# The output layer of four units by seven block products, with sums on VectorE and later operands

## Chip, core and metric

The kernel runs on one core of one Trainium2 chip. The metric is the device time of one execution in microseconds (us). TensorE (PE in the profile) multiplies, ScalarE (ACT) and VectorE (DVE) read its results from PSUM, GpSimd (POOL) works on SBUF alone, and SyncE (SP) issues nearly all DMAs.

## What is computed

Attention inside chunks of 64 rows, then a layer that takes the greatest of three products, then an output layer, all in float32:

```python
# q, k, v: (8, 8, 576, 64); chunks of 64 rows
scores = q_c @ k_c.T / 8;  attn = softmax(scores);  x = attn @ v_c   # x: 4608 x 512
h = np.maximum(np.maximum(x @ w1, x @ w2), x @ w3)                   # 4608 x 768
out = h @ w_out                                                       # 4608 x 512
```

A float32 product is made of three TensorE passes over operands that are split in a high and a low part (function `three`): low times high, high times low, high times high. So each operand costs a copy to the high part (ScalarE) and a subtraction for the low part (VectorE).

## The kernel before

The 4608 rows are 36 tiles of 128. Two groups of four tiles come first; a written order (`FIRST`) runs the first of them beside the weights' loading. The other 28 tiles form four units of 6, 8, 8 and 6 tiles (`UNITS`); I call them units 0 to 3. A unit has a hidden layer and an output layer.

The hidden layer of a unit is done by seven block products in place of eight, for nine sets (three pairs `jp` of hidden blocks, times w1, w2, w3): the tokens of the unit are two halves, the 512 inputs two halves, the pair of hidden blocks two halves. `product(n, i)` makes product `i` of set `n`; the order is 1, 7, (3 of the set before), 6, 2, 4, 5. The seven weight operands of each set are mixed once (`store`) and kept in DRAM, from where `load` brings them to a ring. The seven operands made of the unit's x are made once per unit (`operands`): four differences (`mix`, VectorE makes two and GpSimd two), seven high parts (ScalarE) and seven low parts (VectorE). They are made while TensorE still works on the output layer of the unit before, since the unit's products all need them. Product 6 adds onto the bank of product 1, after ScalarE has copied product 1 out (`kept`).

When w is 2, the greatest values are final: `operand` splits them in a high part (`H`, line 535) and a low part (line 539), 12 pairs per unit, spread over the hidden layer.

The output layer (`project`, line 596) runs plainly: for each tile of 128 tokens six blocks of 128 hidden units, three matmuls of 512 columns each; then ScalarE copies the bank (line 586) and SyncE stores it. Product 3 of the last set runs inside it.

All engines follow one order that the program writes out: `plan(at, pe, fn)` puts a piece of work into a heap with a due time, `passed(step)` advances a clock by the length of each group of matmuls and issues all that is due. So an engine's order is fixed when the program is built, and each engine takes its instructions strictly in that order. `insertion` puts the attention of two further tiles between the matmuls: scores, softmax (VectorE and ScalarE, the scaling by the sum on GpSimd for units 1 to 3), a transpose and the products with v.

Of the kernel before, what the change touches and what calls it, by code (L numbers as in the profile page):

```python
# [9 lines left out]
F32 = mybir.dt.float32  # L10
# [24 lines left out]
OPERANDS, SLOWER = (0.3, 2.0), (1.0, 1.8)  # L35
# [28 lines left out]
def chunk_attn_maxout_kernel(  # L64
# [119 lines left out]
    def three(o, ah, al, bh, bl, first, last, onto=False):  # L184
        nc.tensor.matmul(out=o, lhsT=al, rhs=bh, start=first and not onto, stop=False, skip_group_check=onto)  # L185
        nc.tensor.matmul(out=o, lhsT=ah, rhs=bl, start=False, stop=False, skip_group_check=onto)  # L186
        nc.tensor.matmul(out=o, lhsT=ah, rhs=bh, start=False, stop=last, skip_group_check=onto)  # L187
# [258 lines left out]

    def unit(t0, count, rooms, turn):
# [4 lines left out]
        hh, hl = [None] * JT, [None] * JT  # L452
        stage, m, s = rooms["stage"], rooms["m"], rooms["s"]
# [6 lines left out]
        def room(n):  # L460
            return lambda: s()[:, 2 * n:2 * n + 2, :half]

        b11, b21, b12, b22 = (block(k, c) for c in range(2) for k in range(2))
        source = {1: b11, 2: b21, 3: b22, 4: room(0), 5: room(0), 6: room(1), 7: b12}
# [4 lines left out]
        def high(i):  # L469
            def fn():  # L470
                X[i] = rooms["X"](i)[:, :, :, :half]
                nc.scalar.copy(out=X[i][:, 0], in_=source[i]())
            return fn
# [4 lines left out]
        def operands():  # L478
            return [(0.0, high(1)), (0.6, low(1)), (1.0, high(2)), (1.6, mix(5, b12, b11, nc.vector)), (2.6, low(2)),
                    (2.7, high(5)), (3.6, mix(6, b22, source[5], nc.vector)), (3.7, mix(7, b22, b12, nc.gpsimd)),  # L480
                    (4.6, low(5)), (4.7, high(6)), (5.6, low(6)), (5.8, high(3)), (5.9, mix(4, b21, source[6], nc.gpsimd)),
                    (6.6, low(3)), (6.8, high(7)), (7.6, low(7)), (8.4, high(4)), (9.4, low(4))]
# [20 lines left out]

        def product(n, i):

            jp, w = sets[n]
            a, b = 2 * jp, 2 * jp + 1
            p7 = 2 + 2 * (n % 2)

            def M(j, c):  # L510
                return m()[:, j - a, c, :half]

            def reads(fn):
                def last():
                    fn()
                    give(place)
                return last

            def copy(to):
                return lambda: nc.scalar.copy(out=to, in_=o)  # L520

            def value(k, j, c):
                return lambda: nc.vector.tensor_tensor(out=o if w else M(j, c), in0=o, in1=kept(k), op=plus)  # L523

            def fourth():
                nc.gpsimd.tensor_tensor(out=kept(3) if w else M(b, 1), in0=kept(3), in1=kept(p7), op=plus)  # L526

            def greater(j, c, of):
                return lambda: nc.vector.tensor_tensor(out=M(j, c), in0=of, in1=M(j, c), op=most)  # L529

            def high(j, c):
                def fn():
                    if hh[j] is None:
                        hh[j], hl[j] = (rooms["H"](2 * j + k) for k in range(2))
                    nc.scalar.copy(out=hh[j][:, c * half:(c + 1) * half], in_=M(j, c))  # L535
                return fn

            def low(j, c):
                return lambda: nc.vector.tensor_tensor(out=hl[j][:, c * half:(c + 1) * half], in0=M(j, c),  # L539
                                                       in1=hh[j][:, c * half:(c + 1) * half].bitcast(F32), op=minus)  # L540

            def operand(at, j, c):
                return [(at, high(j, c)), (at + 0.9, low(j, c))] if w == 2 else []

            def summed(k, j, c):
                if w == 0:
                    return [(0.25, reads(value(k, j, c)))]
                return [(0.25, value(k, j, c)), (0.9, reads(greater(j, c, o)))] + operand(2.3, j, c)

            key = n, chain[i]  # L550
            begins = i in (1, 7, 2)
            if begins:
                bank, place = take()
                chains[key] = bank[:, :half], place
            o, place = chains[key]
            if i in (1, 6, 7):
                after = [(0.25, copy(kept({1: 0, 6: 1, 7: p7}[i])))]
            elif i == 5:
                after = [(0.25, copy(kept(3))), (1.2, fourth)]
                after += [(2.5, greater(b, 1, kept(3)))] if w else []  # L560
                after += operand(4.0, b, 1)
            elif i == 2:
                after = summed(0, a, 0)
            elif i == 4:
                after = summed(1, b, 0)
            else:
                after = [(0.25, reads(greater(a, 1, o) if w else copy(M(a, 1))))] + operand(1.6, a, 1)
            for k in range(2):
                hi, lo = weights(n, i, k)
                three(o, hi, lo, X[i][:, 0, k, :half], X[i][:, 1, k, :half], k == 0, k == 1, not begins)  # L570
                yield step, after if k else []
# [9 lines left out]
        def output(tt, of, place):  # L581
            outputs.append(tt)
            o = ao_p.tile([P, DO], F32, name="ao", tag=f"ao{len(outputs) % 4}")
            rows = out[(t0 + tt) * P:(t0 + tt + 1) * P, :]
            if t0 + tt < NT - 1:
                nc.scalar.copy(out=o, in_=of)
                give(place)
                nc.sync.dma_start(out=rows, in_=o)
                return
            left, right = slice(0, 256), slice(256, 512)  # L590
            nc.scalar.copy(out=o[:, left], in_=of[:, left])
            nc.vector.tensor_copy(out=o[:, right], in_=of[:, right])
            nc.scalar.dma_start(out=rows[:, left], in_=o[:, left])
            nc.sync.dma_start(out=rows[:, right], in_=o[:, right])

        def project(*tts, before=JT):
            o, at = {}, {}
            for js in (range(before), range(before, JT)):
                for tt in tts:
                    for j in js:  # L600
                        if j == 0:
                            o[tt], at[tt] = take()
                        cols = slice(tt * P, (tt + 1) * P)
                        three(o[tt], hh[j][:, cols], hl[j][:, cols], woh[:, j, :], wol[:, j, :], j == 0, j == JT - 1)
                        yield STEP, [(0.3, lambda tt=tt: output(tt, o[tt], at[tt]))] if j == JT - 1 else []
                    if tt == 0 and 0 in js and before < JT:
                        yield from product(len(sets) - 1, 3)

        return dict(operands=operands, load=load, hidden=hidden, project=project)
# [94 lines left out]
    H_AT = [(hpool, f"h{k}") for k in range(6)] + [("late", f"k{k}") for k in range(3)]  # L704
    H_AT += [(att, "aa"), (att, "qs"), (att, "rv")]

    def H(k):
        pool, tag = H_AT[k]
        return (late["hold"] if pool == "late" else pool).tile([P, 2 * HALF], F32R, name="H", tag=tag, bufs=1)

    def X(i):
        return hold(("X", i), lambda: late["hold"].tile([P, 2, 2, 512], F32R, name=f"X{i}"))

    rooms = dict(
        stage=stage, X=X, H=H,
        m=lambda: hold("m", lambda: late["hold"].tile([P, 2, 2, HALF], F32, name="most")),
# [72 lines left out]
    def operands(u):  # L789
        if u < len(units):  # L790
            for at, fn in units[u][0]["operands"]():
                plan(now + OPERANDS[min(u, 1)] + SLOWER[min(u, 1)] * at, 0.0, fn)
# [13 lines left out]
    for u, (it, t0, count) in enumerate(units):  # L806
        time = (len(sets) * 14 - 2) * STEP_H[count] + (1.15 if u else 1.65) * sum(UNITS[u + 1:u + 2])
        parts.append(("do", lambda u=u, time=time: series(u + 1, time, 12.0 if u == 0 else 9.0)))
        for n in range(len(sets)):
# [61 lines left out]
```

## Time and profile before

| | |
|---|---|
| Median of 3 runs | 622.86 us (622.02 to 623.68) |
| Profiled execution | 623.29 us, its span 621.5 us |
| PE busy | 612.5 us, 99% of the span |
| DVE, ACT, POOL busy | 59%, 43%, 28% |
| Granted TensorE clock | 1.000 |
| Output layer of units 0, 1, 2, 3 begins at | 250.58, 369.5, 493.7, 592.2 us |

The profile's busy share of PE counts an issued matmul until its modelled end, so starts of consecutive rows give its pace. A group row gives a line, engine, operation, shapes, count, the summed and the mean time, and the idle time ahead of them.

### The profile page before, as it was taken

What the parts mean: (1) busy time and instruction counts of PE and PEld (TensorE: products, weight loads), DVE (VectorE), ACT (ScalarE), POOL (GpSimd) and SP (SyncE); (2) the same over time, 40 slices, a digit from 0 to 9 for tenths busy, and PEclk for the clock granted to TensorE, in tenths of its full rate; (3) what the DMA queues carried; (4) which work ended last, traced back from release to release, by engine and by line L of the source; (5) the groups of instructions that cost most, each with busy time, mean ns of one, the idle gap of its engine ahead of it and who ended that gap; (6) DMA issues with size and microseconds to landing.
All of it is one profiled execution on the core that took longest, in us unless ns stands there. A gap on an engine that the chain in (4) does not pass through costs nothing.

```text
span 621.5 us, 12425 instructions
## 1 busy us (share of the span) xinstructions
PE 612.5 (99%) x5046; PEld 524.5 (84%) x5046; DVE 369.5 (59%) x581; ACT 268.2 (43%) x470; POOL 175.0 (28%) x150
## 2 busy tenths in 40 slices
PE   7899999999999999999999999999999999999997
PEld 3888878887899999888888888888888888999986
DVE  4898965777937665955675669336374480245330
ACT  4887644434444444453344344243343441333321
POOL 2522576786412202422121215002020130111100
PEclk9999999999999999999999999999999999999999
DMA  8987668764958868546788783557758621577402
GB/s 335 359 307 275 234 187 308 257 240 163 373 203 292 322 249 294 201 161 229 253 300 278 255 272 135 170 179 230 253 178 281 215 74 68 185 260 265 138 20 82
DMA packets 56264, 141.06 MB, mean 227 GB/s; under 512 B 5392, under 2 KB 21008, under 8 KB 56208
## 3 DMA queue, kind: packets, MB, share of 16 engines
q1 hardware_dynamic: 56064, 140.14, 63.8%
q8 instruction: 40, 0.66, 0.4%
q14 instruction: 16, 0.13, 0.1%
q10 hardware_dynamic: 144, 0.13, 0.1%
HBM read 110.62 MB, written 29.62 MB: 226 GB/s over the span
## 4 chain that ended last, share of the span: by engine, by line
PE 92%; DVE 6%; ACT 1%; issue 1%; POOL 0%; DVEq 0%; ACTq 0%; POOLq 0%
PE pm L185 28%; PE pm L186 28%; PE pm L187 28%; PE s L235 2%; PE pm L294 2%; PE tp L258 1%; PE pm L660 1%; DVE e L245 1%; DVE s L426 1%; DVE sm L193 1%; DVE mx L240 1%; DVE sm L196 0%; POOL c L418 0%; DVE m L349 0%; DVE xl L305 0%
## 5 line engine op out<-in xcount | busy, mean ns | idle before, releaser
L185 PE MATMUL pm<-X,ring 128*128 128x512 f32 (+1 forms) x504 | 184.2, 365 | 0.0
L187 PE MATMUL pm<-X,ring 128*128 128x512 f32 (+1 forms) x504 | 182.4, 362 | 0.0
L186 PE MATMUL pm<-X,ring 128*128 128x512 f32 (+1 forms) x504 | 182.3, 362 | 0.0
L520 ACT COPY kept<-pm 128x384 f32<-128x384 f32 (+1 forms) x144 | 76.7, 534 | 137.0 <-PE pm L187 134.0
L185 PEld LDWEIGHTS pm<-X,ring 128*128 128x128 f32 x504 | 94.6, 188 | 10.5
L186 PEld LDWEIGHTS pm<-X,ring 128*128 128x128 f32 x504 | 94.7, 188 | 9.8
L187 PEld LDWEIGHTS pm<-X,ring 128*128 128x128 f32 x504 | 94.6, 188 | 9.8
L526 POOL TENSOR_TENSOR kept<-kept 128x384 f32<-128x384 f32 (+1 forms) x24 | 27.7, 1155 | 151.0 <-ACT kept L520 151.0
L523 DVE TENSOR_TENSOR pm<-pm,kept 128x384 f32<-128x384 f32 (+1 forms) x48 | 30.2, 629 | 67.2 <-PE pm L187 67.1
L187 PE MATMUL pm<-woh,H 128*128 128x512 f32 x168 | 65.4, 390 | 0.0
L186 PE MATMUL pm<-wol,H 128*128 128x512 f32 x168 | 65.4, 390 | 0.0
L185 PE MATMUL pm<-woh,H 128*128 128x512 f32 x168 | 65.3, 389 | 0.0
L185 PE MATMUL pm<-xh,wl 128*128 128x512 f32 (+1 forms) x156 | 60.1, 385 | 0.0
L186 PE MATMUL pm<-xl,wh 128*128 128x512 f32 (+1 forms) x156 | 58.4, 374 | 0.3 <-DVE xl L305 0.3
L187 PE MATMUL pm<-xh,wh 128*128 128x512 f32 (+1 forms) x156 | 58.3, 374 | 0.0
L529 DVE TENSOR_TENSOR most<-pm,most 128x384 f32<-128x384 f32 (+1 forms) x72 | 44.9, 623 | 19.7 <-PE pm L187 18.1
L202 POOL TENSOR_TENSOR e<-e,sm 128x512 f32<-128x512 f32 x27 | 31.1, 1153 | 67.5 <-DVE sm L199 36.4
L523 DVE TENSOR_TENSOR most<-pm,kept 128x384 f32<-128x384 f32 (+1 forms) x24 | 14.9, 623 | 58.7 <-PE pm L187 58.6
L526 POOL TENSOR_TENSOR most<-kept 128x384 f32<-128x384 f32 (+1 forms) x12 | 13.8, 1151 | 122.2 <-ACT kept L520 122.2
L539 DVE TENSOR_TENSOR H<-most,H 128x384 fp32r<-128x384 f32 (+1 forms) x48 | 39.6, 829 | 8.7 <-ACT H L535 8.3
L535 ACT CAST H<-most 128x384 fp32r<-128x384 f32 (+1 forms) x48 | 27.3, 569 | 34.5 <-DVE most L529 34.5
L240 DVE TENSOR_REDUCE mx<-s 128x8 f32<-128x512 f32 x36 | 24.6, 683 | 26.5 <-PE s L235 26.5
(95 smaller groups left out, 906.3 us busy)
## 6 DMA issues: line engine op xcount, KB each, us to landing
ring<-w SPq DMA_DIRECT2D x72, 768.0 KB, 5.9
buf<-in_qk SPq DMA_DIRECT2D x36, 512.0 KB, 5.8
buf<-in_vb SPq DMA_DIRECT2D x36, 256.0 KB, 6.5
ring<-w SPq DMA_DIRECT2D x36, 256.0 KB, 3.8
out_x<-ao SPq DMA_DIRECT2D x35, 256.0 KB, 2.0
w<-s SPq DMA_DIRECT2D x9, 768.0 KB, 4.0
stage<-in_w SPq DMA_DIRECT2D x7, 512.0 KB, 5.7
b<-xs SPq DMA_DIRECT2D x14, 256.0 KB, 3.4
```

Source lines behind the costliest of these rows:

```text
L185: nc.tensor.matmul(out=o, lhsT=al, rhs=bh, start=first and not onto, stop=False, skip_group_check=onto)
L186: nc.tensor.matmul(out=o, lhsT=ah, rhs=bl, start=False, stop=False, skip_group_check=onto)
L187: nc.tensor.matmul(out=o, lhsT=ah, rhs=bh, start=False, stop=last, skip_group_check=onto)
L202: eng.tensor_tensor(out=e, in0=e, in1=sm.unsqueeze(2).broadcast_to([P, 8, 64]), op=ALU.mult)
L235: nc.tensor.matmul(out=s[b, c, g, :], lhsT=r[a, 0, 2 * g + h, :], rhs=r[a, 1, 2 * g + h, :], start=True, stop=True)
L240: nc.vector.tensor_reduce(out=st["mx"].rearrange("p (g c) -> p c g", c=2), in_=st["s"], axis=AX.X, op=ALU.max)
L520: return lambda: nc.scalar.copy(out=to, in_=o)
L523: return lambda: nc.vector.tensor_tensor(out=o if w else M(j, c), in0=o, in1=kept(k), op=plus)
L526: nc.gpsimd.tensor_tensor(out=kept(3) if w else M(b, 1), in0=kept(3), in1=kept(p7), op=plus)
L529: return lambda: nc.vector.tensor_tensor(out=M(j, c), in0=of, in1=M(j, c), op=most)
L535: nc.scalar.copy(out=hh[j][:, c * half:(c + 1) * half], in_=M(j, c))
L539: return lambda: nc.vector.tensor_tensor(out=hl[j][:, c * half:(c + 1) * half], in0=M(j, c), in1=hh[j][:, c * half:(c + 1) * half].bitcast ...
```

## The change

The output layer of each unit is done by seven block products as well: the unit's tokens are two halves (3 or 4 tiles each), each pair of hidden blocks two, the 512 output columns two of 256. Each product takes, for each pair `jp` and each tile of its half, three matmuls of 256 columns. The order is `OUT = (1, 2, 6, 7, 5, 4, 3)`.

- The operands made of w_out are mixed once, in unit 0 (`mix_out`): sums on GpSimd, splits on ScalarE and VectorE; two of them go to DRAM (`keep`) and come back for each unit (`out_weights`).
- The sums of hidden values (`sums`): for the first two pairs three on GpSimd and one on VectorE during the hidden layer; for the last pair all four on VectorE, as the output layer begins.
- Splits of hidden values (`split`): seven products times three pairs, 21 pairs of a high and a low part per unit in place of 12; those of product n+2 are due as product n has used its own, since `H` has two rooms per pair.
- Results: products 1, 6, 7 are copied out by ScalarE (line 710), 2, 5, 4 are added to such a copy by VectorE into the store's tile (line 714), 3 is copied by ScalarE (line 712). The stores have rows of 256 columns.
- Operands of the next unit: for units 1 to 3 all four differences are on VectorE; their due times begin 8.5 us (after a unit of 6 tiles) or 12.0 us (after one of 8) into the output layer, in another sequence. The room `mixed` that two differences go through is the same memory as operand X4.
- The last insertion of each unit's hidden layer is due 4.5 us sooner.

Three places show how the engines' orders move. First VectorE, at the change from unit 0 to unit 1: `X` are the seven x operands (the number is the operand's buffer, 2086 is that of product 5, 2126 of 7, 2116 of 3), `kept`, `mixed` and `stage` hold differences. Before, from the second low part of the last hidden values on:

```order
L539 TENSOR_TENSOR H<-most,H 128x384
L476 TENSOR_TENSOR X_2060<-stage,X_2060 128x1024
L467 TENSOR_TENSOR kept<-stage,kept 128x1024
L476 TENSOR_TENSOR X_2086<-kept,X_2086 128x1024
L476 TENSOR_TENSOR X_2108<-kept,X_2108 128x1024
L476 TENSOR_TENSOR X_2116<-stage,X_2116 128x1024
L476 TENSOR_TENSOR X_2126<-stage,X_2126 128x1024
L476 TENSOR_TENSOR X_2142<-kept,X_2142 128x1024
L268 STREAM_TRANSPOSE xs<-e 128x256 x4
```

And now, from the low part for product 6 on:

```order
L527 TENSOR_TENSOR X_2108<-mixed,X_2108 128x1024
L714 TENSOR_TENSOR ao<-pm,kept 128x512
L588 TENSOR_TENSOR H<-most,H 128x384
L714 TENSOR_TENSOR ao<-pm,kept 128x256
L269 STREAM_TRANSPOSE xs<-e 128x256 x2
L588 TENSOR_TENSOR H<-most,H 128x384
L527 TENSOR_TENSOR X_2060<-stage,X_2060 128x1024
L714 TENSOR_TENSOR ao<-pm,kept 128x512
L518 TENSOR_TENSOR stage<-stage,mixed 128x2x512
L714 TENSOR_TENSOR ao<-pm,kept 128x256
L527 TENSOR_TENSOR X_2086<-mixed,X_2086 128x1024
```

The low parts of x stood in one block behind all hidden values; now low parts of hidden values (588) and results (714), both of which the output layer waits for, stand between them.

ScalarE at the same place, up to the first copies of unit 1 (`kept<-pm` of 512 columns). Before:

```order
L472 CAST X_2108<-kept 128x1024
L586 COPY ao<-pm 128x512 x2
L472 CAST X_2116<-stage 128x1024
L586 COPY ao<-pm 128x512
L472 CAST X_2126<-stage 128x1024
L472 CAST X_2142<-kept 128x1024
L586 COPY ao<-pm 128x512 x3
L520 COPY kept<-pm 128x512 x5
```

And now, where X_3558 is operand X4 of unit 1:

```order
L523 CAST X_2060<-stage 128x1024
L585 CAST H<-most 128x384
L523 CAST X_2086<-mixed 128x1024
L523 CAST X_3558<-stage 128x1024
L712 COPY ao<-pm 128x512
L712 COPY ao<-pm 128x256
L523 CAST X_2116<-stage 128x1024
L620 COPY kept<-pm 128x512 x5
```

Between the last high parts of x and the first `kept` copy stood three copies of results; now the high parts of X4 and X3 stand right ahead of it.

GpSimd in unit 0, around the scaling of the softmax of the second insertion (`e<-e,sm`). Before:

```order
L467 TENSOR_TENSOR kept<-stage,kept 128x2x384
L526 TENSOR_TENSOR most<-kept 128x384
L526 TENSOR_TENSOR kept<-kept 128x384
L202 TENSOR_TENSOR e<-e,sm 128x512 x2
L526 TENSOR_TENSOR kept<-kept 128x384
```

And now (`f`, `c` are the mixing of w_out):

```order
L460 TENSOR_TENSOR f<-woh,wol 128x512 x2
L467 TENSOR_TENSOR c<-f 128x256
L467 TENSOR_TENSOR c<-f,c 128x256
L626 TENSOR_TENSOR kept<-kept 128x384
L467 TENSOR_TENSOR c<-f 128x256
L203 TENSOR_TENSOR e<-e,sm 128x512
L467 TENSOR_TENSOR c<-f,c 128x256
L203 TENSOR_TENSOR e<-e,sm 128x512
```

The scaling now stands behind and between the sums of the third mixing, which write the one room `c`.

The diff, cut to its core:

```diff
+OUT = (1, 2, 6, 7, 5, 4, 3)
+OUT_STEP = 0.36
...
+    def mix_out(jp, kept_t3):
...
+                nc.gpsimd.tensor_tensor(out=st["f"][:, k], in0=woh[:, j].bitcast(F32), in1=wol[:, j].bitcast(F32), op=plus)
...
+        return [(0.0, whole(0)), (1.1, whole(1)), (2.2, less(t1, b12, b11)), (2.9, less(t2, b22, t1)),
+                (3.6, less(t3, b22, b12)), (4.3, less(t4, b21, t2)), (8.5, high), (10.5, low), (12.5, keep)]
...
+            start = rooms["start"](turn - 1)
+            return [(start + at, fn) for at, fn in (
+                (0.0, t1), (1.4, t2), (2.6, high(1)), (2.8, t3(nc.vector)), (4.3, low(1)), (4.4, high(7)), (6.2, low(7)),
+                (6.3, high(6)), (8.2, low(6)), (8.3, high(2)), (10.1, low(2)), (11.5, high(5)), (12.0, t4(nc.vector)),
+                (13.9, low(5)), (14.0, high(4)), (15.8, low(4)), (16.2, high(3)), (18.0, low(3)))]
...
+        def split(n, jp):
+            i = OUT[n]
+            def high():
+                H[i, jp] = hpool.tile([P, 2, 512], F32R, name="H", tag=f"h{n % 2 * 3 + jp}")
+                nc.scalar.copy(out=H[i, jp][:, 0, :half], in_=hidden_block(i, jp))
+            def low():
+                nc.vector.tensor_tensor(out=H[i, jp][:, 1, :half], in0=hidden_block(i, jp),
+                                        in1=H[i, jp][:, 0, :half].bitcast(F32), op=minus)
+            return high, low
+        def sums(jp):
...
+            if jp < 2:
+                return [(1.6, lambda: s3(nc.gpsimd)), (2.9, lambda: s1(nc.gpsimd)), (4.2, lambda: s2(nc.vector)),
+                        (5.2, lambda: s4(nc.gpsimd))]
+            high, low = split(2, jp)
+            return [(1.0, lambda: s3(nc.vector)), (1.8, lambda: s2(nc.vector)), (2.8, high), (2.9, lambda: s1(nc.vector)),
+                    (3.6, low), (4.4, lambda: s4(nc.vector))]
...
-        def project(*tts, before=JT):
...
+            def after(i, g):
+                o = held[chain[i], g][0]
+                if i in (1, 6, 7):
+                    return [(0.25, lambda: nc.scalar.copy(out=kept_out(int(i == 6), g), in_=o))]
+                if i == 3:
+                    return [(0.25, stores(g, 0, 1, lambda to: nc.scalar.copy(out=to, in_=o), "x"))]
+                c, d, k, free = {2: (0, 0, 0, "z"), 5: (1, 1, 0, None), 4: (1, 0, 1, "y")}[i]
+                return [(0.25, stores(g, c, d, lambda to: nc.vector.tensor_tensor(out=to, in0=o, in1=kept_out(k, g), op=plus),
+                                      free))]
+            for n, i in enumerate(OUT):
...
+                todo = [(jp, g, q) for jp in range(JT // 2) for g, tiles in enumerate(groups) for q in tiles]
+                if n == len(OUT) - 1:
+                    todo.sort(key=lambda x: (x[1], x[2]))
+                for m, (jp, g, q) in enumerate(todo):
+                    cols, to = slice(q * P, (q + 1) * P), slice(q % 2 * 256, q % 2 * 256 + 256)
+                    three(held[chain[i], g][0][:, to], H[i, jp][:, 0, cols], H[i, jp][:, 1, cols], *of_out(i, jp),
+                          begins and jp == 0 and q % 2 == 0, jp == JT // 2 - 1, True)
...
+    def start(u):
+        return 8.5 if UNITS[u] < 8 else 12.0
...
-            insertion(now + lead + (time - 3.5 - lead) * k / (n - 1), done + k + 1, 14.0 if k == n - 1 else 0.0)
+            insertion(now + lead + (time - (3.5, 8.0)[u > 0] - lead) * k / (n - 1), done + k + 1, 14.0 if k == n - 1 else 0.0)
```

More of the change, by code (lines that the diff above doesn't have):

```diff
@@ L182, in piece, with three @@
         return dict(zip("WABCXHY", (load, exponent, rest, shift, add, high, low)))
[L184 to L187, printed above, removed]
+    def three(o, ah, al, bh, bl, first, last, shared=False):
+        nc.tensor.matmul(out=o, lhsT=al, rhs=bh, start=first, stop=False, skip_group_check=shared)
+        nc.tensor.matmul(out=o, lhsT=ah, rhs=bl, start=False, stop=False, skip_group_check=shared)
+        nc.tensor.matmul(out=o, lhsT=ah, rhs=bh, start=False, stop=last, skip_group_check=shared)
     def over_sum(e):
@@ L520, in copy, with value, greater, operand @@
                 return lambda: nc.scalar.copy(out=to, in_=o)
[L522 to L523 removed]
+            def value(k, q):
+                return lambda: nc.vector.tensor_tensor(out=o if w else M(jp, q), in0=o, in1=kept(k), op=plus)
             def fourth():
[L526 to L545, printed above, removed]
+                nc.gpsimd.tensor_tensor(out=kept(3) if w else M(jp, A22), in0=kept(3), in1=kept(p7), op=plus)
+            def greater(q, of):
+                return lambda: nc.vector.tensor_tensor(out=M(jp, q), in0=of, in1=M(jp, q), op=most)
+            def operand(at, n):
+                return list(zip((at, at + 0.9), split(n, jp))) if w == 2 else []
+            def summed(k, q, n):
                 if w == 0:
[L547 to L548 removed]
+                    return [(0.25, reads(value(k, q)))]
+                return [(0.25, value(k, q)), (0.9, reads(greater(q, o)))] + operand(2.3, n)
+            p7 = 2 + 2 * (n % 2)
             key = n, chain[i]
@@ L579, in hidden @@
                 yield from product(n, i)
[L581 to L594, printed above, removed]
@@ L596, in project @@
-        def project(*tts, before=JT):
[L597 to L607, printed above, removed]
@@ L609, in unit, with out_weights, fn, of_out @@
-        return dict(operands=operands, load=load, hidden=hidden, project=project)
+        def out_weights(k):
+            def fn():
+                ring["out", k] = to = rooms["ring"](turn * len(sets) + last_set, k)
+                nc.sync.dma_start(out=to.bitcast(F32), in_=stored["out"][:, k].rearrange("p a j x -> p (a j) x"))
+            return fn
+        def of_out(i, jp):
+            if i == 7:
+                return [rooms["T3"]()[:, k, jp] for k in range(2)]
+            if i in (5, 4):
+                return [ring["out", (5, 4).index(i)][:, 3 * k + jp] for k in range(2)]
+            j, cols = {1: (2 * jp, slice(0, 256)), 6: (2 * jp, slice(256, 512)), 2: (2 * jp + 1, slice(0, 256)),
+                       3: (2 * jp + 1, slice(256, 512))}[i]
+            return [w[:, j, cols] for w in (woh, wol)]
@@ L611, in chunk_attn_maxout_kernel @@
+        return dict(operands=operands, load=load, hidden=hidden, project=project, out_weights=out_weights)
     starts = [sum(GROUPS[:i]) for i in range(len(GROUPS))]
@@ L703, in chunk_attn_maxout_kernel, with X, M, next_load @@
     late = {}
[L704 to L712, printed above, removed]
+    def X(i, dtype):
+        if dtype == F32:
+            return late["hold"].tile([P, 2, 2, 512], dtype, name="mixed", tag=f"X{i}")
+        make = lambda: late["hold"].tile([P, 2, 2, 512], dtype, name=f"X{i}", tag=f"X{i}")
+        return make() if i == 4 else hold(("X", i), make)
+    def M(n):
+        if n < 6:
+            return hold("M", lambda: late["hold"].tile([P, 6, HALF], F32, name="most"))[:, n]
+        tag = ("aa", "qs", "rv")[n // 2 - 3]
+        return hold(tag, lambda: att.tile([P, 2, HALF], F32, name="most", tag=tag, bufs=1))[:, n % 2]
+    def start(u):
+        return 8.5 if UNITS[u] < 8 else 12.0
+    def next_load(u, k):
+        if u < len(units):
+            units[u][0]["load"](1)[k]()
     rooms = dict(
-        stage=stage, X=X, H=H,
-        m=lambda: hold("m", lambda: late["hold"].tile([P, 2, 2, HALF], F32, name="most")),
+        stage=stage, X=X, M=M, start=start, next=next_load,
+        T3=lambda: hold("T3", lambda: late["hold"].tile([P, 2, 3, 256], F32R, name="T3")),
         s=lambda: hold("s", lambda: late["hold"].tile([P, 5, HALF], F32, name="kept")),
```

142 lines of the change are left out of this document (117 added, 25 removed).

## The prediction

> **What bounds the kernel now.** I read the page first: busy shares and the chain that ended last.
>
> ```profile
> PE 612.5 (99%) x5046; PEld 524.5 (84%) x5046; DVE 369.5 (59%) x581; ACT 268.2 (43%) x470; POOL 175.0 (28%) x150
> PE 92%; DVE 6%; ACT 1%; issue 1%; POOL 0%; DVEq 0%; ACTq 0%; POOLq 0%
> ```
>
> TensorE is the bound. The view of waits from 30 us on, then the table by stages (from..to, length, busy time of PE, PEld, DVE, ACT, POOL, with counts; the output layers of units 0, 1 and 2) show that it hardly ever waits:
>
> ```profile
> PE tp L258 <- DVE e L202: 0.6, 1, 0.6
> 250.58:276.20 25.62, 25.62 (x115) 21.34 (x115) 22.20 (x28) 12.06 (x18) 10.73 (x5) 1.00 0.52 184
> 369.70:404.20 34.50, 34.50 (x153) 28.56 (x153) 23.17 (x27) 13.95 (x20) 10.55 (x5) 1.00 0.46 160
> 494.70:529.40 34.70, 34.70 (x157) 29.02 (x156) 14.14 (x14) 11.91 (x19) 6.15 (x3) 1.00 0.24 85
> ```
>
> So time goes down with matmul columns only while nothing else becomes late. The same rows warn: in unit 0's output layer VectorE is busy 22.2 of 25.6 us already, with 28 instructions.
>
> **What TensorE saves.** The group of the output layer, then TensorE's timeline at 256 columns (27.11 to 31.27) and at 512:
>
> ```profile
> L185 PE MATMUL pm<-woh,H 128*128 128x512 f32 x168 | 65.3, 389 | 0.0
> 27.11 0.39 PE L186 MATMUL pm<-xl,wh 128*128 128x256 f32 x1 [0.34 <-DVE xl L305]
> 27.33 0.28 PE L187 MATMUL pm<-xh,wh 128*128 128x256 f32 x1
> 27.45 0.27 PE L185 MATMUL pm<-xh,wl 128*128 128x256 f32 x1
> ...
> 31.27 0.28 PE L187 MATMUL pm<-xh,wh 128*128 128x256 f32 x1
> 257.62 0.39 PE L187 MATMUL pm<-woh,H 128*128 128x512 f32 x1
> ...
> 275.98 0.39 PE L187 MATMUL pm<-woh,H 128*128 128x512 f32 x1
> ```
>
> Starts give the pace: 32 steps from 27.45 to 31.27 are 0.1194 us each, 81 steps from 257.62 to 275.98 are 0.2267. Before there are 3 x 168 = 504 matmuls of 512 columns, 114.3 us. Now a unit of 6 tiles has 7 x 3 pairs x 3 tiles x 3 = 189 of 256 columns and one of 8 has 252: 882 in all, 105.3 us. **Gain 9.0 us**; a half-size matmul costs 53% of a whole one, so of one eighth (14.3) only that is left. The end gains a little too:
>
> ```profile
> 618.06 0.37 ACT L591 COPY ao<-pm 128x256 f32<-128x256 f32 x1 [3.49 <-PE pm L187]
> 618.47 0.42 DVE L592 COPY ao<-pm 128x256 f32<-128x256 f32 x1 [20.55 <-ACT ao L591]
> 618.92 0.33 SPq L594 DMA_DIRECT2D out_x<-ao  x1
> ```
>
> Two copies of 256 columns follow each other before the last store; now one does. **Gain 0.4.** Transfers I cost at nothing: by the diff's shapes 6 MB more come back for w_out's mixed operands, while the DMA share in the output layers (the last column but one of the stage rows) is 0.24 to 0.52. The cover is that a set's weights are asked for a set ahead; their row of DMA issues (count, size, median time to landing):
>
> ```profile
> ring<-w SPq DMA_DIRECT2D x72, 768.0 KB, 5.9
> ```
>
> **What VectorE gets.** Per unit 9 more low parts of H, 4 sums (one or two of them early), 6 results, and for units 1 to 3 two more differences. The rows for the cost of each, where the distance to the next start counts:
>
> ```profile
> 256.14 0.55 DVE L529 TENSOR_TENSOR most<-pm,most 128x384 f32<-128x384 f32 x1
> 256.61 0.16 DVE L196 TENSOR_SCALAR sm<-sm 128x8 f32<-128x8 f32 x1
> 256.68 1.22 DVE L467 TENSOR_TENSOR kept<-stage 128x1024 f32<-128x1024 f32 x1
> 257.81 0.55 DVE L539 TENSOR_TENSOR H<-most,H 128x384 fp32r<-128x384 f32 x1
> 258.28 0.20 DVE L199 RECIPROCAL sm<-sm 128x8 f32<-128x8 f32 x1
> 258.65 1.16 POOL L202 TENSOR_TENSOR e<-e,sm 128x512 f32<-128x512 f32 x1 [2.11 <-DVE sm L199]
> 258.82 2.07 DVE L476 TENSOR_TENSOR X<-stage,X 128x1024 fp32r<-128x1024 f32 x1
> 272.17 1.41 DVE L268 STREAM_TRANSPOSE xs<-e 128x256 f32<-128x256 f32 x4
> 370.14 0.69 DVE L245 TENSOR_TENSOR e<-s,mx 128x512 f32<-128x512 f32 x1
> 370.75 0.68 DVE L240 TENSOR_REDUCE mx<-s 128x8 f32<-128x512 f32 x1
> 503.17 0.94 DVE L467 TENSOR_TENSOR kept<-stage,kept 128x768 f32<-128x768 f32 x1
> ```
>
> That is 0.47 us for 384 elements, 0.61 for 512, 1.13 for 1024, 1.4 for four transposes; 768 is 0.28 shorter than 1024. A subtraction that meets GpSimd's scaling takes 2.07 in place of 1.22, so a meeting costs 0.85. The Trainium skill (SBUF — State Buffer, "Who interferes with whom") says that a VectorE instruction with two SBUF inputs and a GpSimd instruction that reads SBUF block each other whole; the trace agrees, as 258.65 + 1.16 + 1.13 = 260.94 and the row ends at 260.89. By it the meetings below count 2.6 us in all; without them the sum would be 622.7.
>
> **Unit 0 to 1.** From the start of unit 0's output layer TensorE needs, up to product 6 of unit 1, product 3 (25.62 - 108 x 0.2267 = 1.1), 189 x 0.1194 = 22.6 and 12 x 0.2267 = 2.7: 26.4 us. That product waits for ScalarE's `kept` copy, which stands behind the high parts of X4 and X3; X4 shares memory with `mixed`, so it waits for VectorE's low part of X5 (2086). VectorE's order up to there: 26 instructions of 384 elements (17 low parts, 4 sums, 5 of the last hidden products) 12.2; three results of 512 and three of 256 (0.34, an estimate from 0.61) 2.9; four differences and five low parts of 1024 10.2; transposes 1.4; the softmax's rest 0.9; two meetings 1.7; some five steps that read their predecessor and start at its end (0.55, not 0.47) 0.5: 29.8. ScalarE's rows:
>
> ```profile
> 265.27 1.07 ACT L586 COPY ao<-pm 128x512 f32<-128x512 f32 x2
> 266.22 1.06 ACT L472 CAST X<-stage 128x1024 fp32r<-128x1024 f32 x1
> 267.17 0.59 ACT L586 COPY ao<-pm 128x512 f32<-128x512 f32 x1
> ```
>
> So two high parts at 0.95, two copies (0.48 and some 0.3) and `kept` at 0.59: 3.2 more. 33.0 against 26.4: TensorE waits about **6.5 us**, part of it inside the output layer (product 3 accumulates onto the bank that VectorE's result of product 5 reads) and the rest at unit 1's product 6. Bounds: 3.5 if VectorE arrives without backlog and meets no scaling, 8 with a third meeting.
>
> **Unit 1 to 2.** GpSimd's sum there takes 1.3:
>
> ```profile
> 370.45 1.30 POOL L526 TENSOR_TENSOR kept<-kept 128x512 f32<-128x512 f32 x1 [10.47 <-ACT kept L520]
> ```
>
> The low part that comes last is H for product 3's third pair. TensorE reaches it after 6 x 0.2267 + 222 x 0.1194 = 27.9 us. VectorE until then: 28 instructions of 512 elements (17 low parts, 4 sums, 3 of the last hidden products, 4 results) 17.1, four differences and four low parts 9.0, transposes 1.4, softmax 0.9, a meeting 0.9, a wait of 1.3 for GpSimd's sum of the last set, steps 0.5: 31.1. **Wait 3 us**, bounds 1 and 5. **Unit 2 to 3**: eight of the 1024s are 768 now (-2.2), no insertion is left (-2.3): 26.6, under 27.9, **no wait**. After unit 3 no operands follow: none.
>
> **Unit 0's hidden layer.** GpSimd mixes w_out there; two scalings now stand among these sums.
>
> ```profile
> 234.44 1.05 POOL L202 TENSOR_TENSOR e<-e,sm 128x512 f32<-128x512 f32 x1 [9.24 <-DVE sm L199]
> 236.41 1.05 POOL L202 TENSOR_TENSOR e<-e,sm 128x512 f32<-128x512 f32 x1
> 238.09 0.60 PE L258 MATMUL tp<-ident,e 128*128 128x128 f32 x4
> ```
>
> A scaling ends 2.6 us before TensorE's transpose (235.49 to 238.09). In the new order three sums (`c`, 128x256) and one of `kept` stand ahead of it, and the sums wait until VectorE has read the room `c`, itself behind a softmax. That is about 2.6 plus **1.5 us**, between 0 and 3. **Restarts**: after a wait TensorE's next start came 0.22 later, not 0.12 (27.11, 27.33); some eight waits cost 0.8.
>
> **Sum**: -9.0 - 0.4 + 6.5 + 3 + 1.5 + 0.8 = +2.4. The profiled execution (623.29, span 621.5 and 1.8 around it) becomes 625.7; it was 0.4 above the median of the runs, so I forecast 622.86 + 2.4 = **625.3 us**.
>
> **Rivals.** (1) *VectorE keeps up*, and the change is faster: one mechanism, its backlog at the first two borders. If VectorE is free as the output layer begins and no scaling meets it, the two waits are 3.5 + 1 and the time is some 618; with no wait at all it is 622.86 - 9.4 = 613.5. The point from which no wait is left is VectorE's 29.8 us falling under 26.4 - 3.2 = 23.2. For it: before, the stage rows leave VectorE 3.4 us of slack in unit 0's output layer, and 11.3 and more in the later ones. Against: the counts are fixed by the order. (2) *The clock drops.* The first rows run at half pace:
>
> ```profile
> 1.19 5.73 PE L660 MATMUL pm<-h 128*128 128x512 bf16 x13 [1.19 <-DVE h L662]
> 18.56 0.66 PE L258 MATMUL tp<-ident,e 128*128 128x128 f32 x4 [1.16 <-POOL e L202]
> ```
>
> 13 matmuls in 5.7 us are 0.44 each against 0.2267. If a wait at unit 1's start brings that back for as long, it costs about 2.9 us more: 628. Against it: after 1.16 us of waiting at 18.56 the pace was whole. The Trainium skill (TensorE: Matmul & The Clock Gate, "Part 1") puts the limit at an idle window of about 3.4 us, which the longest wait here would come near only if the 6.5 fell together. (3) *Weight loads set the pace* at 256 columns:
>
> ```profile
> L185 PEld LDWEIGHTS pm<-X,ring 128*128 128x128 f32 x504 | 94.6, 188 | 10.5
> ```
>
> At 188 ns each, 882 are 166 us, 52 more than before. The rows at 0.1194, which load weights each time, speak against it.
>
> **How the numbers follow.** Forecast 0.70 (621 to 629.5), VectorE keeps up wholly or half 0.20 (613.5 to 620.5), clock 0.06, a late transfer 0.02 (some +3), weight loads 0.02. A measurement of this kernel can tell about 0.3% (1.9 us) from no change. Slower: 0.52 of the forecast and the last three, 0.62; within: 0.18 and 0.05, 0.23; faster 0.15. The range, 618.5 to 630, leaves out 0.13 below and 0.06 above.
>
> **What would show it.** Right: 882 matmuls about 0.12 apart; waits of TensorE for VectorE's H and results near the end of the output layers of units 0 and 1, for ScalarE's `kept` at unit 1's start, none in units 2 and 3; VectorE without idle time there. Wrong: a TensorE without waits after 250 us (rival 1), rows of 0.44 us after a wait (2), or 256-column starts 0.19 apart (3).

## The result, and the profile after

| | before | after |
|---|---|---|
| Median | 623.00 us (622.02 to 623.68, 4 runs) | 632.73 us (628.97 to 633.59, 4 runs) |
| Profiled execution, its span | 623.29, 621.5 | 633.59, 631.6 |
| Granted TensorE clock, mean of the span | 1.000 | 0.992 |

The ratio is 1.0146, with a 95% interval of 1.0102 to 1.0189: the change makes the kernel slower by some 9.7 us, where the forecast was 2.4 and the range ended at 630. The page of the changed kernel, busy times and the chain that ended last:

```profile
PE 610.7 (97%) x5424; PEld 539.8 (85%) x5424; DVE 419.0 (66%) x682; ACT 290.8 (46%) x522; POOL 202.4 (32%) x186
PE 77%; DVE 14%; DMA 3%; ACT 2%; issue 2%; POOL 1%; SPq 0%; ACTq 0%; DVEq 0%; POOLq 0%
```

TensorE is still the bound, but 14% of the chain are VectorE's and 3% a DMA's, where 6% and none were before. The stages tell where. From the table by stretches, first matmul of a stage to first matmul of the next (the last stage to the span's end), in us:

| unit | hidden layer before | after | output layer before | after |
|---|---|---|---|---|
| 0 | 77.01 | 84.10 | 25.63 | 26.96 |
| 1 | 93.32 | 97.92 | 34.01 | 35.54 |
| 2 | 90.13 | 90.17 | 34.01 | 31.61 |
| 3 | 64.51 | 64.49 | 29.31 | 27.36 |

Units 2 and 3 show the gain by itself: 2.40 and 1.95 us, with no wait. Units 0 and 1 lose 14.6 us, and most of it (7.1 and 4.6) not in the output layers, which were changed most, but in the hidden layers. The rows of those two stages before and after (columns as in the stage rows shown with the prediction; the clock is the last column but two):

```profile
173.57:250.58 77.01, 77.01 (x918) 75.49 (x916) 42.46 (x82) 34.99 (x71) 14.29 (x14) 1.00 0.75 268
276.21:369.53 93.32, 93.32 (x886) 77.36 (x884) 54.18 (x92) 36.19 (x63) 16.68 (x14) 1.00 0.77 259
```

```profile
173.46:257.56 84.10, 78.94 (x917) 76.67 (x916) 50.98 (x96) 37.22 (x80) 37.83 (x39) 0.98 0.76 269
257.56:284.52 26.96, 24.55 (x197) 23.91 (x196) 26.86 (x45) 15.38 (x29) 3.06 (x3) 1.00 0.46 148
284.52:382.44 97.92, 95.24 (x887) 78.47 (x885) 57.55 (x100) 36.56 (x63) 25.23 (x21) 0.98 0.80 274
```

TensorE's busy time is 5.2 us short of the stage in unit 0's hidden layer, and the clock is 0.98. VectorE is busy 26.86 of 26.96 us in unit 0's output layer, as forecast. What TensorE waited for from 150 us on (engine, tile and line, what it waited for: us in total, times, longest):

```profile
PE tp L259 <- ACT xs L264: 3.7, 1, 3.7
PE pm L186 <- DVE H L588: 2.5, 2, 1.7
PE pm L186 <- ACT kept L620: 2.1, 1, 2.1
PE tp L259 <- POOL e L203: 1.5, 1, 1.5
PE pm L186 <- DVE ao L714: 1.4, 1, 1.4
PE pm L186 <- ACT stage L887: 0.6, 1, 0.6
```

**The largest wait was not forecast at all.** ScalarE's timeline in unit 0's hidden layer, and behind it SyncE's and TensorE's of the same stretch:

```profile
194.68 0.48 ACT L620 COPY kept<-pm 128x384 f32<-128x384 f32 x1 [1.51 <-PE pm L188]
203.16 0.71 ACT L479 CAST s<-c 128x256 fp32r<-128x256 f32 x2 [7.99 <-DMA wo<-s]
...
204.39 0.57 ACT L264 COPY xs<-tp 128x512 f32<-128x512 f32 x1
```

```profile
193.29 1.30 SPq L489 DMA_DIRECT2D wo<-s  x2
194.69 5.52 SPq L551 DMA_DIRECT2D ring<-w  x3
```

```profile
198.68 0.66 PE L259 MATMUL tp<-ident,e 128*128 128x128 f32 x4 [1.49 <-POOL e L203]
205.10 1.09 PE L259 MATMUL tp<-ident,e 128*128 128x128 f32 x4 [3.67 <-ACT xs L264]
```

`mix_out` writes the pieces of w_out's mixed operands into the tile `s`, which has one room. The high part of the next pair waits until the store of the pair before (issued at 193.29) has landed, and that took until 203. ScalarE works in order, so the copy of a transpose (204.39), which needs nothing of this, stood behind it, and TensorE behind that. Between 188 and 206 us the transfers kept the DMA engines busy 94% of the time (queue: packets, MB, share):

```profile
q1 hardware_dynamic: 2316, 6.05, 93.6%
wo<-s SPq DMA_DIRECT2D x4, 256.0 KB, 6.6
```

**And the clock fell, three times.** The table by stretches of 3.41 us, which is how long each stretch at half clock lasts (from..to, length, PE busy with its count, granted clock, DMA share, GB/s), each with the stretch ahead of it:

```profile
201.23:204.64 3.41, 0.20 (x2) 1.00 1.01 416
204.64:208.06 3.42, 2.96 (x11) 0.50 0.56 205
...
286.57:289.98 3.41, 1.32 (x6) 1.00 1.06 394
289.98:293.39 3.41, 3.41 (x10) 0.50 0.49 158
409.44:412.86 3.42, 1.71 (x11) 1.00 0.37 116
412.86:416.27 3.41, 3.41 (x16) 0.50 0.80 185
```

In all three, a stretch in which TensorE was busy for half of the time or less is followed by one at half the clock. By the granted clock such a stretch does the work of 1.7 us in 3.4, so each costs some 1.7 (an estimate), and three 5.1.

At the change of unit 0 to 1 TensorE waited at the places that were forecast. ScalarE's timeline there:

```profile
286.23 1.05 ACT L523 CAST X<-stage 128x1024 fp32r<-128x1024 f32 x1 [6.55 <-DVE X L527]
287.18 0.85 ACT L712 COPY ao<-pm 128x512 f32<-128x512 f32 x2
287.92 1.06 ACT L523 CAST X<-stage 128x1024 fp32r<-128x1024 f32 x1
288.87 1.08 ACT L620 COPY kept<-pm 128x512 f32<-128x512 f32 x2
```

The last of VectorE's queue ahead of it, the low part of X5:

```profile
284.97 1.22 DVE L527 TENSOR_TENSOR X<-mixed,X 128x1024 fp32r<-128x1024 f32 x1
```

X4's high part waits 6.55 us for that (they share a room), then come two copies of results, X3 and at last `kept`, which TensorE's product 6 had waited for since 287.4.

**The books**, by stages: the gain of matmuls and tail some -8.6 (2.4 in unit 2 and as much in unit 1, 1.95 with the tail in unit 3, some 1.8 in unit 0, the last an estimate: unit 3's without the tail, which gave 0.13, from 3.91 to 3.78 us between TensorE's last start and the span's end); the change of unit 0 to 1 +5.1 (waits of 1.4, 0.8, 2.1 and 0.2, with the restarts behind them), that of 1 to 2 +1.9 (1.7 and its restart); GpSimd's scaling +1.5; the store's landing +3.7; ScalarE's copy to `stage` at 376.98 in unit 1's hidden layer +0.6, which was not forecast either; the clock +5.1. Together +9.3; the spans differ by 10.1. The 0.8 that is left was not followed up. A part of it is that a wait is counted from a matmul's modelled end: the one of 1.42 us that ends at 279.99 puts 1.70 between two starts that are else 0.12 apart.

### The profile page after: what moved, and what is told of

Read it like the earlier page. It is cut to its first block, busy times and chain, and to the rows that moved or that the text cites. A ratio compares the mean times of both kernels' runs of the same rounds, so it can differ in the third digit from the quotient of the medians.

```text
span 631.6 us, 13484 instructions
## 1 busy us (share of the span) xinstructions
PE 610.7 (97%) x5424; PEld 539.8 (85%) x5424; DVE 419.0 (66%) x682; ACT 290.8 (46%) x522; POOL 202.4 (32%) x186
## 4 chain that ended last, share of the span: by engine, by line
PE 77%; DVE 14%; DMA 3%; ACT 2%; issue 2%; POOL 1%; SPq 0%; ACTq 0%; DVEq 0%; POOLq 0%
PE pm L186 24%; PE pm L187 23%; PE pm L188 23%; DVE H L588 3%; PE s L236 2%; PE pm L295 2%; DMA wo<-s 1%; PE tp L259 1%; DVE e L246 1%; DVE X L527 1%; DVE mx L241 1%; DMA buf<-in_vb 1%; DVE sm L194 1%; PE pm L793 1%; DMA b<-xs 1%
## 5 line engine op out<-in xcount | busy, mean ns | idle before, releaser
L188 PEld LDWEIGHTS pm<-X,ring 128*128 128x128 f32 x504 | 95.2, 189 | 10.1
L588 DVE TENSOR_TENSOR H<-most,H 128x384 fp32r<-128x384 f32 (+1 forms) x72 | 50.9, 713 | 8.8 <-ACT H L585 8.8
L585 ACT CAST H<-most 128x384 fp32r<-128x384 f32 (+1 forms) x72 | 40.5, 568 | 33.5 <-DVE most L629 22.1
L186 PE MATMUL pm<-woh,H 128*128 128x256 f32 x168 | 48.9, 291 | 4.0 <-DVE H L588 2.5
L187 PE MATMUL pm<-wol,H 128*128 128x256 f32 x168 | 48.2, 287 | 0.0
L188 PE MATMUL pm<-woh,H 128*128 128x256 f32 x168 | 48.2, 287 | 0.0
L186 PEld LDWEIGHTS pm<-woh,H 128*128 128x128 f32 x168 | 32.9, 196 | 5.1 <-DVE H L588 3.1
```

What stands on the lines that cost most here:

```text
L186: nc.tensor.matmul(out=o, lhsT=al, rhs=bh, start=first, stop=False, skip_group_check=shared)
L585: nc.scalar.copy(out=H[i, jp][:, 0, :half], in_=hidden_block(i, jp))
L588: nc.vector.tensor_tensor(out=H[i, jp][:, 1, :half], in0=hidden_block(i, jp), in1=H[i, jp][:, 0, :half].bitcast(F32), op=minus)
```

## The experiments

The theory after the trace: the change is slower because ScalarE stands behind a store's landing, because VectorE's order puts operand work ahead of values that TensorE needs sooner, and because each long wait brings a stretch at half clock. The rivals: VectorE has too much to do in any order; the clock falls for another reason; taking a wait away only uncovers the next.

**e1_rooms: a room of its own for each pair's `s`.**

```
-  st["s"] = att.tile([P, 2, 2, 256], F32R, name="s", tag="aa", bufs=1)
+  if jp: st["s"] = hpool.tile([P, 2, 2, 256], F32R, name="s", tag=f"h{3 + jp}")
+  else:  st["s"] = att.tile([P, 2, 2, 256], F32R, name="s", tag="aa", bufs=1)
```

> The changed kernel, with a room of its own for the pieces of w_out's mixed operands that go to DRAM: pairs 1 and 2 use the rooms of H that are not in use yet, so ScalarE's high part no longer waits until the store of the pair before has landed. Theory: ScalarE's 7.99 us of idle time ahead of that high part at 203.16, and with it TensorE's wait of 3.67 us for the transposes' copy at 205.10, go, and so does the stretch of 3.4 us at half clock behind it (another 1.7): the hidden layer of unit 0 falls from 84.1 to about 79, the time from 632.7 to about 627.5; the wait of 1.5 us for GpSimd's scaling at 198.68 stays. Rival: the copy is late for another reason (GpSimd's sums or VectorE's low parts stand ahead of it), and the time stays at 632 or so. Second rival: the stretch at half clock has nothing to do with the wait, so only 3.7 go: 629.

Measured: 627.01 us (626.63 to 628.67), ratio to before 1.0065 (1.0048 to 1.0082). Unit 0's hidden layer is 80.05 us, the wait for the transposes' copy is gone and there is no stretch at half clock there; those at 284.78 and 407.66 stayed. 5.7 us less than the changed kernel's 632.73, against 5.2 expected: the store's landing and the clock behind it were more than half of the 9.7 that the change lost.

**e2_late: X2, X5, X4, X3 of the next unit behind the results.**

```
-  (6.3, high(6)), (8.2, low(6)), (8.3, high(2)), (10.1, low(2)), (11.5, high(5)), (12.0, t4(nc.vector)),
-  (13.9, low(5)), (14.0, high(4)), (15.8, low(4)), (16.2, high(3)), (18.0, low(3))
+  (6.3, high(6)), (8.2, low(6)), (13.9, high(2)), (16.4, low(2)), (16.8, high(5)), (17.6, t4(nc.vector)),
+  (18.4, low(5)), (18.6, high(4)), (19.6, low(4)), (21.2, high(3)), (22.8, low(3))
```

> The changed kernel, with nothing removed: only the due times of the x operands X2, X5, X4, X3 of units 1 to 3 (high and low parts, and one difference) are put behind the last hidden values and results of the output layer, since the next unit's products need them 1.5 to 8 us after its start. Theory: TensorE's waits at the changes of unit 0 to 1 and 1 to 2 (5.2 and 2.5 us) come from VectorE's order, where 5 to 6 us of operand work stands ahead of H's low parts, results and ScalarE's copy; they fall to 2 to 4 us in all, and the stretches at half clock behind them go (1.7 each): 624 to 627 in place of 632.7. Rival: VectorE's amount of work sets it, and what is put off makes the next unit's first products wait as long: 630 or more, with the waits in the first 10 us of units 1 and 2.

Measured: 629.75 us (629.35 to 631.88), ratio 1.0118 (1.0100 to 1.0135): 3.0 us less than the changed kernel, where 5.7 to 8.7 were expected, and just short of the rival's 630. Unit 1's output layer is 31.76 us in place of 35.54, without a wait, but then product 6 of unit 2 waits 3.2 us for ScalarE's `kept`. ScalarE's timeline shows why:

```profile
409.75 0.59 ACT L712 COPY ao<-pm 128x512 f32<-128x512 f32 x1 [4.94 <-DMA out_x<-ao]
411.91 1.05 ACT L523 CAST X<-stage 128x1024 fp32r<-128x1024 f32 x1 [1.57 <-DVE X L527]
414.88 0.58 ACT L712 COPY ao<-pm 128x512 f32<-128x512 f32 x1 [1.93 <-DMA out_x<-ao]
```

The copy of a result waits for a room, that is for a store to land: the pattern of `s` again, with another tile. So the rival was right in that a wait took the place of the one removed, but it was for the most part a store and not VectorE's amount of work. Two stretches at half clock are gone (one is left, at 203.94): the 3.2 us fell on two stretches of 3.41, 1.77 in the one and 1.39 in the next, and neither sufficed. The waits themselves did not fall as the theory said: at the two changes they add up to 6.6 us (0.2, 1.4, 0.8, 1.0 and 3.2), and in the changed kernel to 6.2 (0.2, 1.4, 0.8, 2.1 and 1.7). What was won is about the price of the two stretches, 3.4 us. That VectorE's order is a cause is shown by e3_early, e5_order and e9_both below, not by this run.

**e3_early: the same operands sooner**, `8.5` and `12.0` in `start` replaced by `2.0` and `5.5`.

> The changed kernel with 'later' undone in part: the x operands of units 1 to 3 are due 6.5 us sooner, everything else as it is. Theory: operand work then stands ahead of more of H's low parts, so the output layers of units 0 and 1 wait more and sooner: 634 to 640. Rival: the late start is what makes the operands late for the next unit, and a sooner one takes the waits away: 625 to 629.

Measured: 639.82 us (637.55 to 641.01), ratio 1.0268 (1.0245 to 1.0291), as the theory said. TensorE waits 8.2 us for H in six places (2.5 in two in the changed kernel) and five stretches of 3.41 us run at half clock. Later operands are thus a part of the change that helps; they don't go far enough.

**e4_dose: waits of several lengths in the kernel before.**

```
+  again = 0 if i != 1 else {1: (0, 5, 7, 6, 8, 7, 6, 9, 7), 2: (0, 6, 8, 7, 5, 6, 7, 8, 9)}.get(turn, [0] * 9)[n]
-  after = [(0.25, copy(kept({1: 0, 6: 1, 7: p7}[i])))]
+  after = [(0.25, copy(kept({1: 0, 6: 1, 7: p7}[i])))] * (1 + again)
```

> The kernel before, in which ScalarE's copy of product 1 is repeated 5 to 9 times in sets 1 to 8 of units 1 and 2, so that TensorE's product 6 waits in 16 places for about 1 (5 repeats) to 3.5 us (9 repeats), with nothing else changed. Theory: a stretch of 3.41 us at half clock follows where TensorE stood idle for some two thirds of the 3.41 us before it: no such stretch after the waits of about 1 us, nearly always after those over 3, in between it depends on where the wait falls on the grid of 3.41 us. Rival 1: only a whole stretch of 3.41 us without work brings it: none after waits under 3.4. Rival 2: waits have nothing to do with it, and the clock stays at 1.000 as in the kernel before. Some 40 us slower in all by the waits, up to 20 more by the clock.

Measured: 677.73 us (one run), clock 0.972: TensorE waited 34.3 us for `kept` in 14 places, and eleven stretches of 3.41 us ran at half clock. The table by stretches, four times a stretch with a wait and the one behind it:

```profile
312.00:315.41 3.41, 1.69 (x8) 1.00 0.37 150
315.41:318.83 3.42, 3.42 (x105) 1.00 0.02 5
325.66:329.07 3.41, 0.85 (x4) 1.00 1.00 400
329.07:332.48 3.41, 3.02 (x7) 0.50 0.85 296
339.31:342.72 3.41, 1.34 (x6) 1.00 1.03 337
342.72:346.13 3.41, 3.19 (x8) 0.50 0.32 87
...
479.26:482.67 3.41, 2.32 (x11) 1.00 0.63 217
482.67:486.08 3.41, 3.41 (x17) 1.00 0.00 0
```

The kernel before has a clock of 1.000, so the waits brought the drops: rival 2 falls. Rival 1 falls as well, since no stretch here was without work: in 339.31 TensorE was busy 1.34 us. Over all ten profiled executions with the change or with doses, on the grid of 3.41 us that the starts of the stretches give: of the stretches at full clock, all 18 with 1.97 us or more without a matmul were followed by one at half clock, of 8 with 1.71 to 1.88 us five were, and none with 1.47 or less. A stretch that is itself at half clock was followed by another with 1.11, 1.49 and 1.66 us already, and once (409.76 in e6_pool) with 0.39. So the same wait costs 1.7 us more or not, by where it falls on the grid. The changed kernel's executions differ by 4.6 us: the fastest, 628.97, has a mean clock of 0.997, and 633.30 and 633.59 have 0.992; but 632.16 has 0.989, so the clock is not all of that difference.

**e6_pool: two differences back on GpSimd** (from e1_rooms).

```
-  (2.8, t3(nc.vector))
+  (2.8, t3(nc.gpsimd))
...
-  (12.0, t4(nc.vector))
+  (12.0, t4(nc.gpsimd))
```

> The kernel e1_rooms (627.0), with the two differences for X7 and X4 of units 1 to 3 on GpSimd again, due as before; the hidden sums stay on VectorE. Theory: a difference takes GpSimd 3.4 us where it meets VectorE (before, at 250 to 280) against 1.13 on VectorE, and locks VectorE meanwhile, so the waits at the changes of unit stay or grow: 627 to 631. Rival: VectorE's count of instructions alone sets the waits; two fewer per change are 2.3 us less each for two changes, and a stretch at half clock less: 620 to 623.

Measured: 631.94 us (631.45 to 632.96), ratio 1.0142 (1.0128 to 1.0155): 4.9 us slower than e1_rooms, a little past what the theory gave, and the rival falls. GpSimd's difference took 6.76 us, not 3.4 (GpSimd's timeline, then VectorE's):

```profile
264.98 6.76 POOL L521 TENSOR_TENSOR stage<-stage 128x1024 f32<-128x1024 f32 x1 [7.49 <-DVE mixed L521]
281.48 2.40 POOL L521 TENSOR_TENSOR stage<-stage,mixed 128x1024 f32<-128x1024 f32 x1 [9.74 <-DVE X L530]
```

```profile
264.82 1.02 DVE L591 TENSOR_TENSOR H<-most,H 128x384 fp32r<-128x384 f32 x2
265.75 1.22 DVE L521 TENSOR_TENSOR mixed<-stage,mixed 128x1024 f32<-128x1024 f32 x1
266.89 1.02 DVE L591 TENSOR_TENSOR H<-most,H 128x384 fp32r<-128x384 f32 x2
...
268.96 0.55 DVE L591 TENSOR_TENSOR H<-most,H 128x384 fp32r<-128x384 f32 x1
273.26 0.56 DVE L591 TENSOR_TENSOR H<-most,H 128x384 fp32r<-128x384 f32 x1 [3.75 <-ACT H L588]
```

VectorE's instructions beside it keep their lengths, so it is GpSimd that stood still: VectorE's row ends at 269.51, and GpSimd's instruction 2.23 us later, nearly the 2.40 that it took at 281.48. There it was the other way round, and VectorE's low part of X at 282.19 took 2.78 us in place of 1.22. X7's high part waits for it on ScalarE, the high parts of H stand behind that, VectorE runs dry for 3.75 us, and TensorE waits 3.2 us in the output layer. A part of the 4.9 is the clock: three stretches at half clock against two in e1_rooms. That VectorE makes these differences is right, at least in this order of its work.

**e7_nolow: VectorE eased** (from e1_rooms), the low parts of X left out of `operands` for units 1 to 3.

> The kernel e1_rooms (627.0), which leaves out the seven low parts of the x operands of units 1 to 3: TensorE multiplies with the high part twice, so it has as much to do, and VectorE 7 x 1.13 = 7.9 us less per change of unit. Theory: with VectorE eased the waits at both changes (5.2 and 2.5 us) and both stretches at half clock (1.7 each) go but for a rest of 1 to 2 us: 616 to 618.5. Rival: ScalarE's queue (high parts and copies) or the stores hold TensorE at the changes as well: 622 or more.

Measured: 619.04 us (618.75 to 620.13), ratio 0.9931 (0.9916 to 0.9946): 8.0 less than e1_rooms, 0.5 short of the range expected. No stretch at half clock is left. VectorE's load is thus a cause as well: with 7.9 us less of it at each change the waits nearly go. 1.0 us for `kept` and 0.8 for H remain, so this part does not hang on the low parts of X (the 0.8 is gone in e9_both).

**e8_mix: w_out's second and third pair mixed later** (from e1_rooms), `0.5 + 7.0 * jp` replaced by `(0.5, 8.0, 16.5)[jp]`.

> The kernel e1_rooms (627.0), with w_out's second and third pair mixed 0.5 and 2 us later and nothing else changed. Theory: TensorE's wait of 1.4 us for GpSimd's scaling near 198 in unit 0 goes, since the sums of that pair no longer stand ahead of it: 625.5. Rival: the sums meet another scaling and the wait only moves: 627.

Measured: 625.68 us (625.42 to 627.02), ratio 1.0043 (1.0030 to 1.0057), the 625.5 that the theory gave, though the interval overlaps with that of e1_rooms. The trace is clearer: the wait for GpSimd's scaling is gone, and one of 0.7 us for VectorE came in its place; unit 0's hidden layer is 78.26 us.

**e5_order: all of it together**, with due times of the operands for each unit and a fifth room for results (`(3, 1, 2, 3, 0, 4, 1, 2)[len(outputs) % 8]` in place of `len(outputs) % 4`).

> All of the change is kept, and the order of what stands beside it is written anew: the room of its own from e1_rooms; w_out's second and third pair mixed 0.5 and 2 us later, so that no three sums stand ahead of GpSimd's scaling; a fifth room for results, so that ScalarE's copy need not wait for a store (4.94 us at 409.75 in e2_late); X1, X7, X6 of the next unit early in the output layer and X2, X5, X4, X3 behind its results. Theory: the waits of TensorE that the change brought (3.7, 1.5, 5.2 and 2.5 us) fall to 3 to 4 us in all, none of them fills half of a stretch of 3.41 us, so that no stretch at half clock comes; the gain of 9.4 on matmuls and tail stands against that: 616 to 619, faster than the kernel before by 0.6 to 1.1%. Rival: VectorE's amount of work in the output layers of units 0 and 1 sets the end whatever the order: 623 or more.

Measured: 620.54 us (619.86 to 622.13), ratio 0.9958 (0.9946 to 0.9971): faster than the kernel before, with a clock of 1.000, but 1.5 us short of the range expected. TensorE's longest waits (the changed kernel has neither the first nor the last, but e1_rooms has the last too):

```profile
PE pm L186 <- DMA ring<-w: 1.2, 1, 1.2
PE pm L186 <- ACT stage L890: 0.9, 1, 0.9
PE pm L186 <- DVE H L591: 0.8, 1, 0.8
PE pm L187 <- DVE X L530: 0.7, 1, 0.7
```

**e9_both: three edits against these waits, and two shifts of due times.**

```
-  (8.5, high), (10.5, low), (12.5, keep)
+  (8.5, high), (10.5, low), (18.0, keep)
-  if n == len(OUT) - 1:
+  if n == len(OUT) - 1 and turn == len(UNITS) - 1:
```

The third edit puts high(5) ahead of low(2). The shifts: the third pair is mixed another 1.0 us later, and unit 2's operands are due another 0.5 us later.

> The kernel e5_order (620.5), with three edits for the waits that are left in it: the stores of w_out's mixed operands are asked for 5.5 us later (in e5_order the loads of unit 0's weights stood behind one of them on SyncE, and TensorE waited 1.2 us for such a load at 201.43); product 3 of the output layer goes by tiles in unit 3 alone, and by pairs of hidden blocks in units 0 to 2, so that the third pair's values are needed 0.7 us later (TensorE waited 0.8 us for H there, near 277); X5's high part ahead of X2's low part. Theory: these waits go: 618 to 619.5, faster than the kernel before by 0.6 to 0.8%. Rival: the waits move to VectorE's next instructions, since its queue in unit 0's output layer is full: 620 or more.

Measured: 618.86 us (617.25 to 620.00, 6 runs), ratio 0.9922 (0.9906 to 0.9937): 4.2 us faster than the kernel before, the fastest of all, and within the range expected. Its stages for unit 0 and unit 1's output layer:

```profile
173.32:252.89 79.57, 77.55 (x917) 75.40 (x916) 55.46 (x96) 37.65 (x82) 39.14 (x39) 1.00 0.82 293
252.89:278.74 25.85, 25.00 (x196) 24.06 (x196) 25.75 (x45) 15.33 (x30) 3.06 (x3) 1.00 0.40 126
...
372.77:404.38 31.61, 31.61 (x259) 31.35 (x258) 30.14 (x46) 18.59 (x29) 3.13 (x3) 1.00 0.41 130
```

Unit 1's output layer has its full gain (34.01 to 31.61) with VectorE busy 95% of it. What is left is mostly in unit 0's hidden layer: 79.57 us against 77.01 before (and 0.7 us for `stage` in unit 1's). There a wait of 0.7 to 1.4 us near 200 remains in each of these versions, for GpSimd, a load or VectorE in turn; why it always finds a successor was not settled. Unit 0's output layer gains nothing either (25.85 against 25.63), with VectorE busy for 25.75 of it: there the amount of VectorE's work may be the limit, and no run settled it (e7_nolow, with VectorE eased, takes 25.16). The single worth of the fifth room and of each edit of e9_both was not measured.

## Why the prediction was wrong

The direction was right, and so were the places of the waits that came from VectorE's order, at sizes a little too high. But two causes that stood outside the sum made 8.8 us: the wait for a store, priced at nothing (a late transfer had a chance of 0.02), and the clock, a rival with a chance of 0.06. Without them the books come to +0.5 (-8.6 + 5.1 + 1.9 + 1.5 + 0.6), or +1.3 with the 0.8 left open, too little to tell from no change. So "slower" came out right mostly by luck.

- **Matmuls**: right in the pace, a little too high in the sum. TensorE's timeline in unit 0's output layer shows 12 steps of 0.12 each; gain and tail measured some 8.6, against 9.4, of which the tail gave 0.13 and not 0.4.

```profile
282.72 0.28 PE L186 MATMUL pm<-woh,H 128*128 128x256 f32 x1
...
284.16 0.28 PE L186 MATMUL pm<-woh,H 128*128 128x256 f32 x1
```

- **Unit 0 to 1, 6.5**: 4.5 measured (5.1 with the restarts, which the sum had apart), at the places named: results, H and `kept` behind X4 and X3. VectorE's order up to the end of X5's low part took 28.6 us (257.56 to 286.19), against 29.8.
- **Unit 1 to 2, 3**: 1.7 measured (1.9 with the restart), for H of the output layer's last product, as named. Unit 2 to 3 and unit 3: none, as forecast.
- **GpSimd's scaling, 1.5**: 1.49 measured at 198.68; e8_mix shows that it was the sums ahead of it.
- **The step that failed first** is "Transfers I cost at nothing". It weighed loads by their share of the DMA engines in the output layers. But the new stores are in unit 0's hidden layer, where that share is 0.76, and their price is not bytes but a room: ScalarE, which takes its instructions in the program's order, waits for a landing (7.99 us), and TensorE behind it (3.67). For `mix_out` I priced GpSimd's sums and not ScalarE's high parts, though the room `s` with `bufs=1` stands in the diff. e1_rooms: 5.7 us with the clock behind it.
- **The second** is the rival on the clock: "after 1.16 us of waiting at 18.56 the pace was whole" was read as evidence against it, and the price was for one drop only. e4_dose and the nine other executions show that up to 1.47 us without a matmul in one stretch never brought a drop and 1.97 or more always did; three came, at some 1.7 each, not one at 2.9. The Trainium skill (TensorE: Matmul & The Clock Gate, "Part 1") speaks of an idle window of about 3.4 us that runs freely. By that rule I took it that a wait near 3.4 us was needed. The grid agrees, the idle window does not: busy for 1.34 of 3.41 us was not enough to keep the clock.
- **Rival 1** (VectorE keeps up, 613.5 to 620.5; its 618 leaves out the 1.5 for GpSimd's scaling, and is 619.5 with it) did not come, but e9_both lies inside it at 618.9, with all of VectorE's work. In unit 1 the order, not the amount, was thus the limit; in unit 0's output layer that stays open.

## What to carry to other kernels

Before a change adds a store, look for who writes that tile next: if it is an engine with other work behind it, a room with one buffer puts the landing time (here 4 to 9 us beside loads) into that engine's queue. Order work for the next stage by when it is first needed, with values of the running stage ahead of it. On a kernel that TensorE bounds, a wait of 2 us costs 2 or, with a stretch at half clock behind it, some 3.7, so price each wait with the clock, and judge several executions, since it depends on the grid.

## What the runs showed of the hardware that was not expected

- The clock falls to half for 3.41 us, at times for two such stretches in a row, behind a stretch of 3.41 us in which TensorE was idle for some 1.7 to 1.9 us or more (18 of 18 from 1.97 on, 5 of 8 between 1.71 and 1.88, none up to 1.47); a wait of 3.2 us split over two stretches did nothing.
- GpSimd's 128x1024 subtraction took 2.40 us at 281.48 in e6_pool, where VectorE's instruction at 282.19 was held up (2.78 in place of 1.22), 3.4 in the kernel before, and 6.76 at 264.98 beside a gapless row of VectorE subtractions, which themselves did not slow down. Before, GpSimd's scaling had held VectorE up by 0.85. The Trainium skill (SBUF — State Buffer, "Who interferes with whom") says that whichever of the two issues first has the shared ports and the other is blocked; the traces agree on both kinds of victim, and e6_pool adds that a gapless row of VectorE kept GpSimd out until the row's end at 269.51.
